# A fused attention, MoE and SwiGLU kernel whose order of work comes from a planner: new durations, lags and due times, the single block last, another order of the seven products

## The chip, the cores and the metric

The kernel runs on one core of a Trainium2 chip. The metric is the device time of one execution in microseconds (us). Inputs and outputs are in device memory; nothing is done on the host.

## What is computed

Three stages follow each other on 4608 tokens of width 512. In the reference:

```python
# 1: linear attention, q, k, v of 8 batches x 8 heads x 576 x 64
q_s = softmax(q, axis=-1); k_s = softmax(k, axis=2)      # over the head's 64, over the 576 rows
kv = einsum('bhsd,bhse->bhde', k_s, v)
x = einsum('bhsd,bhde->bhse', q_s, kv)                   # then heads beside each other: 4608 x 512
# 2: hard swish
h = x @ w_in                                             # 512 -> 2048
y = (h * clip(h + 3, 0, 6) / 6) @ w_out                  # 2048 -> 512
# 3: RMS norm and SwiGLU
xn = y / sqrt(mean(y * y) + 1e-6) * rms_g
out = (silu(xn @ w_gate) * (xn @ w_val)) @ w_out2        # 512 -> 1536 -> 512
```

The softmaxes subtract the maximum first. The four weight matrices arrive as 64-bit floats; the kernel makes 32-bit floats of them with integer operations.

## The kernel before, in words

**Tiling.** The tokens are nine blocks (j = 0 to 8) of 512 columns; the chunks of a width are 128 rows. Each product of two 32-bit matrices is done by three passes of TensorE: operands are split into a high part (a copy into a rounded type by ScalarE, `hi_of`, L201) and a low part (the difference, a tensor_tensor of VectorE or GpSimd, `lo_of`, L207), and high x high, high x low and low x high are added up in PSUM.

**Stages on TensorE.** `m1` (L600) makes h for blocks 0 to 2 with plain products; `prod1` (`product`, L830) makes it for blocks 3 to 8 with seven products in place of eight (a Strassen-Winograd scheme on 256-column halves). `m2` (L659) makes y: 16 steps of 12 matmuls a block. `prod` (L848) makes gate and value for "supers", blocks taken in pairs (two columns of the scheme are two blocks, 512-column matmuls) or a single one (256-column halves). There are 6 chunk pairs i and two matrices z in a super, so 12 groups of seven products; a product is 6 matmuls. `m4` (L968) makes the output: 12 steps of 12 matmuls a block. Before the change the supers are `(0,), (1,2), (3,4), (5,6), (7,8)`.

**The seven products.** They are done in `ORDER` = 1, 6, 5, 2, 7, 3, 4 and accumulate in three PSUM banks x, y, z. Between them sums are taken from PSUM: p1 (ScalarE copies bank x after 1, L863), u2 (VectorE adds bank y after 6, L870), v (VectorE adds bank z after 5), c22 (v plus bank y after 7), c12 and c21. Product 2 waits for p1, 7 for u2, 3 for v, 4 for c22. `merge` strews other steps between the seven: two steps stand behind the fourth and the seventh product, four behind the second, fourth, sixth and seventh.

**The written order of TensorE.** `seq` is a list of all steps of `m1`, `m2`, `prod1`, `prod` and `m4`. In prod1, a block's `m2` steps follow its products by four chunks, and its last four stand in the first group of the next block. In prod, the list `wait` of the m4 steps (super by super, block by block) is eaten two steps a group, whenever the chunks that they need were made by an earlier group; what remains stands at the end.

**The planner.** `Plan` is a list scheduler that runs when the program is built. Every piece of work is a task with an engine, a duration in us, a due time (a place in `seq`), needs, a lag until its result is seen by another engine, and what it takes and gives of pools of buffers ("u": 77 tiles of 128x512; "w": 8 tiles twice as wide; "ps": 4 PSUM banks; "v", "vt", "st"). `emit` goes through simulated time, and gives each free engine the ready task with the smallest due time. The simulated time itself is then forgotten: what remains in the program is the order of instructions on each engine, and that each engine takes them in this order. A VectorE task may go to GpSimd where `other` says so (FLEX), and a task with `port` keeps the two engines apart in the plan. All DMAs are issued by SyncE, in the plan's order; a DMA task lasts 0.73 us there and has a lag of `DMA_LAG` = 2.3 us.

**Attention side work.** `kv_tasks` makes a batch's key-value product: five loads of k, `k_max` (L347: a tensor_reduce over the four rows of a partition; the tail rows L353), a transpose on TensorE (`k_tr`, L363), `k_red` (L367 the maximum of each column; L369 a product with the identity, "kd"), `k_all` (L375: ones x kd, which gives the maximum to all partitions), `k_ev` (L379, ScalarE), `k_sub`, `k_exp`, `kv_mm` (L408), `kv_div`. `q_tasks` makes the query's side: `q_max1` (L500), `q_exp1` (L506), sums (L511, L512), `q_norm` (L516), `q_tr` (L528), and the x products (L548, L556). The norm of block j is `y_ev` (L672, L674: the four PSUM banks of y are copied out, which the next block's first `m2` waits for), squares and sums, `y_sum` (L689) and `y_newton` (L700 to L703).

**Weights.** `weight` plans the conversion of one 128x512 piece: a load into a "w" tile, `conv_a` (two ScalarE operations, L245 and L246), `conv_d` (on VectorE, four operations each in two halves of 256 columns: L254, L256, L258, L262), `conv_p` (L267, GpSimd first) and `conv_s` (L271). There are 68 pieces: "in" 16, "out" 16, "gv" 24 (gate and value), "out2" 12. The 36 last are due one after the other from the first `m2` of block 2 to the fourth group of block 8's prod1; an "out2" piece is then stored (`w_put`) and loaded again (`w_get`) in the prod stage, and split there (`v_hi`, `v_lo`). For the supers of two blocks, the x of the prod stage is loaded into "w" tiles (`load_xn`), 1024 columns at a time.

Of the kernel before, what the change touches and what calls it, by code (L numbers as in the profile page):

```python
# [20 lines left out]
UNITS = 98 - 5 - 2 * WIDE  # L21
# [6 lines left out]
LAG = 3  # L28
SOLO_US, WORTH = 0.2, 0.6
XP = 4  # L30
# [6 lines left out]
class Plan:  # L37
# [5 lines left out]

    def __init__(self, room):
        self.room = dict(room)
        self.tasks = {}

    def add(self, name, engine, us, fn, *args, needs=(), due=0.0, take=(), give=(), spare=0, lag=0.1, other=None, port=True):
        assert name not in self.tasks, name
        self.tasks[name] = (engine, us, fn, args, list(needs), due, dict(take), dict(give), spare, lag, other, port)  # L50

    def emit(self):
# [25 lines left out]
        while len(begun) < len(self.tasks):  # L78
            for engine, heap in ready.items():
# [3 lines left out]
                while heap:  # L83
# [4 lines left out]
                    first, us, fn, args, _, _, take, give, spare, lag, other, port = self.tasks[name]  # L88
# [30 lines left out]
            while events and events[0][0] <= now:  # L119
                _, _, name, far, give = heapq.heappop(events)  # L120
                for p, n in give.items():
                    self.room[p] += n
                for u in users[far].get(name, ()):
                    left[u] -= 1
                    if not left[u]:
                        arm(u)
# [3 lines left out]
def kernel(  # L130
# [35 lines left out]
    SUPER = [(0,), *((j, j + 1) for j in range(1, NJ, 2))]  # L166
    COUPLES = ((1, 6), (5, 2), (7, 3), (4,))
# [26 lines left out]
    g_sb = const.tile([P, C], F32, name="g_sb")  # L194

# [43 lines left out]
    HS = [slice(z * NB // 2, (z + 1) * NB // 2) for z in range(2)]  # L239
# [9 lines left out]
    def conv_d(kind, i):  # L249
# [7 lines left out]
        for h in HS:  # L257
            nc.vector.scalar_tensor_tensor(  # L258
                wi[:, h], t[:, h, 1], -(1 << 30), mi[:, h], ALU.bitwise_and, ALU.bitwise_or
            )  # L260
        for h in HS:
            nc.vector.tensor_scalar(mi[:, h], wi[:, h], -(1 << 23), None, ALU.bitwise_and)  # L262
# [79 lines left out]
    def k_max(b, u):  # L342
# [3 lines left out]
        if u < C:  # L346
            nc.vector.tensor_reduce(  # L347
                m[:, u * P:(u + 1) * P].rearrange("p (h d) -> p h d", h=2),
                kch[b, u].rearrange("p (h t d) -> p h d t", h=2, t=T),
                AX.X, ALU.max,  # L350
            )
        else:
            nc.vector.tensor_max(m[:TAIL], m[:TAIL], kch[b, u][:TAIL])  # L353
# [11 lines left out]
    def k_red(b):  # L365
        m = stat.tile([P, C, 1], F32, tag="kx", bufs=2, name=f"kx{b}")
        nc.vector.tensor_reduce(m, kmp.pop(b), AX.X, ALU.max)  # L367
        kms[b] = utile(f"kd{b}", F32, (P, C, P))
        nc.vector.tensor_tensor(  # L369
            kms[b], ident.rearrange("p (o q) -> p o q", o=1).to_broadcast([P, C, P]), m.to_broadcast([P, C, P]), ALU.mult  # L370
        )

    def k_all(b):
        kmp[b] = ptile(f"kmb{b}")
        nc.tensor.matmul(kmp[b], ones, kms.pop(b).rearrange("p c q -> p (c q)"), start=True, stop=True)  # L375

    def k_ev(b):
        kms[b] = utile(f"kmb{b}")
        nc.scalar.copy(kms[b], kmp.pop(b))  # L379
# [355 lines left out]
    ORDER = (1, 6, 5, 2, 7, 3, 4)  # L735
# [142 lines left out]
    def load_xn(S, k, t):  # L878

        n = f"b{k + 1}{t + 1}"  # L880
        if len(SUPER[S]) == 2:
            x = wtile(f"x{n}_{S}", F32, (P, 2, NB))
            src = xn_d[SUPER[S][t]][2 * k:2 * k + 2]
        else:
            x = utile(f"x{n}_{S}", F32, (P, 2, HALF))
            src = xn_d[SUPER[S][0]][2 * k:2 * k + 2, :, t * HALF:(t + 1) * HALF]
        nc.sync.dma_start(x, src.rearrange("c p t -> p c t"))
        xb["u", S, n] = x

    def u_sum(S, n, x, y, eng):  # L890

        to = {"t3": "b12", "t4": "t2"}.get(n)
        if to:
# [593 lines left out]
```

## Time and profile before

| what | us |
|---|---|
| time of three executions | 1794.81 median (1789.85 to 1899.04) |
| the profiled execution | 1790.45 |
| its span, from the first to the last instruction | 1788.6 |
| TensorE busy in the span | 1711.6 |
| VectorE busy | 1303.7 |
| ScalarE busy | 870.0 |
| GpSimd busy | 260.1 |

The profile is of one execution. The mean granted clock of TensorE in it was 0.988 of full speed. Busy shares are taken over the whole span; waits and windows of the trace show the stretches. The matmul durations of the rows overlap each other, so a busy TensorE need not be one without a loss.

### The profile page before, as it was taken

The page shows a single profiled execution, that of the slowest core. Times are in us where ns is not written, and L with a number is a line of the kernel's source. Part 1 is how long each engine was busy: PE and PEld are TensorE (multiplying, and loading weights), DVE is VectorE, ACT ScalarE, POOL GpSimd, SP SyncE. Part 2 cuts the span into 40 slices and gives each one's busy share as a digit, 9 for nine tenths or more (in the row PEclk, how much of TensorE's full clock was granted, in tenths as well). Part 3 has the DMA queues.
Part 4 walks back from the last instruction along what each step waited for, and adds up shares of the span by engine and source line. Part 5 has one row for each costly group of instructions (what it writes and reads, how often), then busy time and mean ns, then how long its engine had stood idle before and what let it go on. Part 6 is the DMA issues. An engine that isn't in the chain of part 4 may idle for free.

```text
span 1788.6 us, 26411 instructions
## 1 busy us (share of the span) xinstructions
PE 1711.6 (96%) x9150; PEld 1445.5 (81%) x9150; DVE 1303.7 (73%) x2501; ACT 870.0 (49%) x2018; POOL 260.1 (15%) x259
## 2 busy tenths in 40 slices
PE   5899989999999999999999989999999999999999
PEld 3677767888888788898988878878887888788887
DVE  8898977887887888887877786676557655665552
ACT  7865555564564656544546553343234323433331
POOL 3244411021111211121110010020002000100000
PEclk9899999999999999999999999999999999999999
DMA  9547386895887979686793745344354444544443
GB/s 262 174 142 238 115 292 207 308 320 194 269 260 237 269 233 309 213 274 217 266 321 113 244 134 184 109 159 167 122 166 164 159 135 151 173 150 139 147 148 129
DMA packets 192294, 358.27 MB, mean 200 GB/s; under 512 B 26145, under 2 KB 90145, under 8 KB 192161
## 3 DMA queue, kind: packets, MB, share of 16 engines
q1 hardware_dynamic: 192160, 356.59, 61.3%
q8 instruction: 72, 1.18, 0.3%
q14 instruction: 62, 0.50, 0.1%
HBM read 288.88 MB, written 67.63 MB: 199 GB/s over the span
## 4 chain that ended last, share of the span: by engine, by line
PE 74%; DVE 12%; DMA 8%; ACT 3%; issue 2%; SPq 1%; POOL 0%; DVEq 0%; ACTq 0%; POOLq 0%
PE y L659 16%; PE o L968 16%; PE puy L848 12%; PE pux L848 8%; PE puz L848 8%; PE phy L830 4%; PE h L600 3%; PE phz L830 3%; PE phx L830 2%; DMA q<-in_q_dram 2%; DMA raw_gv<-in_moe_w_val_dram 2%; PE kvp L408 2%; DMA raw_out<-in_moe_w_out_dram 1%; ACT q L506 1%; DMA v<-in_v_dram 1%
## 5 line engine op out<-in xcount | busy, mean ns | idle before, releaser
L968 PE MATMUL o<-wv,uh 128*128 128x512 f32 x864 | 267.2, 391 | 0.0
L207 DVE TENSOR_TENSOR plu<-pg,phu 128x512 fp32r<-128x512 f32 (+1 forms) x232 | 149.1, 647 | 122.0 <-ACT phu L201 121.8
L968 PEld LDWEIGHTS o<-wv,uh 128*128 128x128 f32 x864 | 162.4, 189 | 33.2
L968 PE MATMUL o<-wv,ul 128*128 128x512 f32 x432 | 168.7, 390 | 1.0 <-DVE ul L207 1.0
L659 PE MATMUL y<-gh,hout 128*128 128x512 f32 x360 | 144.9, 403 | 10.2 <-DVE ysb L674 9.5
L863 ACT COPY c21u<-pux 128x512 f32<-128x512 f32 (+1 forms) x60 | 32.6, 543 | 241.8 <-PE pux L848 241.7
L659 PE MATMUL y<-gl,hout 128*128 128x512 f32 x360 | 142.6, 396 | 6.2 <-DVE gl L207 5.8
L201 ACT ACTIVATE phu<-pg 128x512 fp32r<-128x512 f32 x240 | 133.5, 570 | 23.1 <-DMA pg<-pd 23.0
L659 PE MATMUL y<-gh,wo 128*128 128x512 f32 x432 | 142.8, 391 | 0.0
L659 PE MATMUL y<-gh,lout 128*128 128x512 f32 x360 | 141.8, 394 | 0.0
L848 PE MATMUL puy<-xhu,phu 128*128 128x512 f32 (+1 forms) x360 | 134.3, 373 | 7.7 <-DVE c22u L870 7.6
L848 PE MATMUL puy<-xlu,phu 128*128 128x512 f32 (+1 forms) x360 | 132.6, 368 | 0.0
L848 PE MATMUL puy<-xhu,plu 128*128 128x512 f32 (+1 forms) x360 | 132.4, 368 | 0.0
L870 DVE TENSOR_TENSOR c22u<-c22u,puy 128x512 f32<-128x512 f32 (+1 forms) x60 | 38.0, 633 | 128.9 <-PE puy L848 128.7
L830 PE MATMUL phy<-xhh,wh 128*128 128x256 f32 x576 | 118.6, 289 | 0.0
L830 PEld LDWEIGHTS phy<-xhh,wh 128*128 128x128 f32 x576 | 95.2, 192 | 3.1 <-issue 1.5
L935 POOL TENSOR_TENSOR u<-u,c12u 128x512 f32<-128x512 f32 x19 | 30.6, 1608 | 458.2 <-DVE c12u L870 286.4
L968 PEld LDWEIGHTS o<-wv,ul 128*128 128x128 f32 x432 | 81.4, 188 | 18.6 <-DVE ul L207 1.5
L659 PEld LDWEIGHTS y<-gh,wo 128*128 128x128 f32 x432 | 81.3, 188 | 15.9
L506 ACT ACTIVATE q<-q,qm 128x64 f32<-128x64 f32 x256 | 85.2, 338 | 15.7 <-DVE qm L500 12.7
L848 PE MATMUL pux<-xlu,phu 128*128 128x512 f32 (+1 forms) x240 | 89.1, 371 | 2.0 <-DVE xlu L207 2.0
L848 PE MATMUL pux<-xhu,phu 128*128 128x512 f32 (+1 forms) x240 | 89.0, 371 | 1.5 <-ACT c21u L863 0.9
(252 smaller groups left out, 4573.8 us busy)
## 6 DMA issues: line engine op xcount, KB each, us to landing
wh<-rdh SPq DMA_DIRECT2D x126, 512.0 KB, 5.2
wv<-rdout SPq DMA_DIRECT2D x96, 512.0 KB, 4.7
pg<-pd SPq DMA_DIRECT2D x180, 256.0 KB, 3.7
wo<-rdout SPq DMA_DIRECT2D x54, 512.0 KB, 4.3
raw_out<-in_moe_w_out_dram SPq DMA_DIRECT2D x28, 512.0 KB, 5.3
rdh<-hw SPq DMA_DIRECT2D x21, 512.0 KB, 4.1
v<-in_v_dram SPq DMA_DIRECT2D x72, 128.0 KB, 5.4
xn_d<-ysb SPq DMA_DIRECT2D x36, 256.0 KB, 4.2
```

Source lines behind the costliest of these rows:

```text
L201: nc.scalar.activation(hi, src, AF.Copy)
L207: on(engine).tensor_tensor(lo, src, hi.bitcast(F32), ALU.subtract)
L408: nc.tensor.matmul(ps[e * D:(e + 1) * D, u, s:s + D + 1], kk, vv, start=(u == 0 and t == 0), stop=(t == T), skip_group_check=True,)
L506: nc.scalar.activation(t, t, AF.Exp, bias=m[:, g, :], accum_out=sm[:, g, :])
L600: nc.tensor.matmul(hps[j, i], w[a][:, o:o + P], xs[j][b][u], start=(u == 0 and m == 0), stop=(u == C - 1 and m == 2),)
L659: nc.tensor.matmul(acc[j][c], w[a][:, c * P:(c + 1) * P], g[b], start=(i == 0 and n == 0), stop=(i == NF - 1 and n == 2),)
L830: nc.tensor.matmul(ps[:, z, :], w[a][:, o:o + P], x[b][:, c * HALF:(c + 1) * HALF], start=(first and z == 0 and c == 0 and m == 0), stop=( ...
L848: nc.tensor.matmul(ps, w[a][:, c * P:(c + 1) * P], x[b][c], start=(first and c == 0 and m == 0), stop=(c == 1 and m == 2), skip_group_chec ...
L863: nc.scalar.copy(cs[l, j, i, "c21"], bank(l, j, i, "x"))
L870: nc.vector.tensor_tensor(cs[l, j, i, n], t, bank(l, j, i, b), ALU.add)
L935: on(eng).tensor_tensor(u, u, c_part("u", S, (i, 1), m, t, 0), ALU.mult)
L968: nc.tensor.matmul(acc["o", j][c], u[a][:, c * P:(c + 1) * P], w[b], start=(i == 0 and n == 0), stop=(i == NF2 - 1 and n == 2),)
```

## The change

It changes the planner's figures, the list `seq`, and a few pieces of computation:

- Planner: `DMA_LAG` 2.3 to 4.0 (and 2 more for loads of q and v), default lag 0.1 to 0.15, TensorE lag 0.2 to 0.25; several durations (conv_d 1.88 to 1.55, conv_a 1.06 to 1.13, GpSimd's 1.23 to 1.35, kv_div 1.25 to 1.48 and others). A task may have `slack`: it is made ready that long after its needs are met. The attention's TensorE tasks from batch 3 (block 3) on get 0.8 us of it (`SIDE`), and `y_sum` too.
- First block: q, v, the first weights and the first query maxima have earlier due times.
- `SUPER` is `(0,1), (2,3), (4,5), (6,7), (8,)`. Block 1 of the first pair fetches its w_out2 parts from device memory as later blocks do.
- `ORDER` is 1, 6, 5, 7, 2, 3, 4, with `COUPLES` to match, and `merge` has fixed places: two steps stand behind the third and the sixth product, four behind the third, fifth, sixth and seventh.
- `m2` follows prod1 by six chunks (`TRAIL`), and no m4 step is given to the last three groups (`REST`).
- "out2" weights are loaded and converted from 30 steps before their first use, without store and second load. "gv" weights are due over a longer stretch, to 16 steps before the last pair's first group in the first super.
- `conv_d` works on whole 512 columns.
- `k_max` takes two tensor_max (256 and 128 columns a partition) in place of the reduce. `k_red` keeps only the maximum; `k_all` is four transposes of the maximum, broadcast along the free axis.
- x of the prod stage is loaded, summed and split in 512-column tiles of the "u" pool, which has 76 tiles now.

```diff
-UNITS = 98 - 5 - 2 * WIDE
+UNITS = 97 - 5 - 2 * WIDE
+SIDE = 0.8
+TRAIL = 6
+REST = 3
...
-                    if not left[u]:
+                    if left[u]:
+                        continue
+                    if self.tasks[u][12]:
+                        heapq.heappush(events, (now + self.tasks[u][12], serial, u, 2, {}))
+                        serial += 1
+                    else:
                         arm(u)
...
-    SUPER = [(0,), *((j, j + 1) for j in range(1, NJ, 2))]
-    COUPLES = ((1, 6), (5, 2), (7, 3), (4,))
+    SUPER = [tuple(range(j, min(j + 2, NJ))) for j in range(0, NJ, 2)]
+    COUPLES = ((1, 6), (5, 7), (2, 3), (4,))
...
-        for h in HS:
-            nc.vector.tensor_scalar(m[:, h], m[:, h], F64_MIN, F64_MAX, ALU.max, ALU.min)
-        for h in HS:
-            nc.vector.tensor_scalar(mi[:, h], mi[:, h], 3, 0x3FFFFFFF, ALU.logical_shift_left, ALU.bitwise_and)
...
+        nc.vector.tensor_scalar(m, m, F64_MIN, F64_MAX, ALU.max, ALU.min)
+        nc.vector.tensor_scalar(mi, mi, 3, 0x3FFFFFFF, ALU.logical_shift_left, ALU.bitwise_and)
+        nc.vector.scalar_tensor_tensor(wi, t[:, :, 1], -(1 << 30), mi, ALU.bitwise_and, ALU.bitwise_or)
+        nc.vector.tensor_scalar(mi, wi, -(1 << 23), None, ALU.bitwise_and)
...
-            nc.vector.tensor_reduce(
-                m[:, u * P:(u + 1) * P].rearrange("p (h d) -> p h d", h=2),
-                kch[b, u].rearrange("p (h t d) -> p h d t", h=2, t=T),
-                AX.X, ALU.max,
-            )
+            t4 = kch[b, u].rearrange("p (h t d) -> p h t d", h=2, t=T)
+            nc.vector.tensor_max(km2, t4[:, :, :T // 2], t4[:, :, T // 2:])
+            nc.vector.tensor_max(m[:, u * P:(u + 1) * P].rearrange("p (h d) -> p h d", h=2), km2[:, :, 0], km2[:, :, 1])
...
-        nc.tensor.matmul(kmp[b], ones, kms.pop(b).rearrange("p c q -> p (c q)"), start=True, stop=True)
+        for c in range(C):
+            nc.tensor.transpose(kmp[b][:, c, :], m[:, c, :].to_broadcast([P, P]), ident)
...
-    ORDER = (1, 6, 5, 2, 7, 3, 4)
+    ORDER = (1, 6, 5, 7, 2, 3, 4)
...
-        out = []
-        for n, p in enumerate(ps):
-            out.append(p)
-            out += ms[n * len(ms) // len(ps):(n + 1) * len(ms) // len(ps)]
-        return out
+        at = {2: (2, 5), 4: (2, 4, 5, 6), 6: (1, 2, 3, 4, 5, 6)}.get(len(ms), range(len(ms)))
+        return [x for n, p in enumerate(ps) for x in (p, *(m for m, a in zip(ms, at) if a == n))]
...
-            late = [(m2, j, i) for i in range(4 * p - 4, 4 * p)] if p else tail2[j - 1]
+            late = [(m2, j, i) for i in range(max(0, 4 * p - TRAIL), 4 * p - TRAIL + 4)] if p else tail2[j - 1]
...
-    FLEX = (G, 1.23)
-    DMA_US, DMA_LAG = 0.73, 2.3
+    FLEX = (G, 1.35)
+    DMA_US, DMA_LAG = 0.73, 4.0
...
-            plan.add((n, "put"), Q, DMA_US, w_put, *n, needs=[(n, "s")], due=d, give=U, lag=DMA_LAG)
-            plan.add((n, "get"), Q, DMA_US, w_get, *n, needs=[(n, "put"), *late[1]], due=h - 5, take=U, spare=5, lag=DMA_LAG)
-            split((n,), [(n, "get"), *step(h - 8)], h - 4, v_hi, v_lo, (i,), first={"w": 1}, take=(), give=U, other=FLEX)
+            split((n,), [(n, "s"), *step(h - 8)], h - 4, v_hi, v_lo, (i,), first={"w": 1}, take=(), give=U, other=FLEX)
...
-            plan.add(have[b], Q, 2 * DMA_US if two else DMA_US, load_xn, S, k, t,
-                     needs=[(y, "store", 2 * k), (y, "store", 2 * k + 1), *step(e - 14)], due=e - 10,
-                     take=R, spare=0 if two else SPARE // 2, lag=DMA_LAG)
+                plan.add(b, Q, DMA_US, load_xn, S, k, t, c,
+                         needs=[*((y, "store", 2 * k + m) for m in ([c] if two else [0, 1])), *step(e - 16)], due=e - 11,
+                         take=U, spare=SPARE // 2, lag=DMA_LAG)
...
+        first, last = pos[m2, 2, 0], pos[prod, 0, NP2 - 1, 0, 1] - 16
+        for z, (m, c) in enumerate(((1, 0), (1, 1), (0, 0), (0, 1))):
+            d = first + (last - first) * (4 * i + z) // (4 * NP2)
+            weight("gv", (i, m, c), pos[prod, 0, i, 0, 1], step(d - 20), (d, ()))
+        for ch in (i, i + NP2):
+            h = pos[m4, 0, 0, ch]
+            weight("out2", ch, h, step(h - 30), (h - 12, ()))
```

## Rows read from the trace of the kernel before

**Rows 1.** The page's first part: busy time, share, instructions of each engine.
```profile
PE 1711.6 (96%) x9150; PEld 1445.5 (81%) x9150; DVE 1303.7 (73%) x2501; ACT 870.0 (49%) x2018; POOL 260.1 (15%) x259
```

**Rows 2.** Stages by windows: length, then busy time (count) by engine, clock, DMA.
```profile
0.00:36.80 36.80, 18.24 (x110) 11.44 (x110) 29.68 (x65) 26.91 (x92) 10.59 (x36) 1.00 1.04 268
36.80:146.00 109.20, 96.67 (x526) 75.16 (x524) 101.43 (x238) 75.34 (x225) 40.27 (x36) 0.92 0.54 163
...
358.00:940.00 582.00, 563.79 (x3713) 500.40 (x3712) 477.47 (x1014) 322.99 (x823) 99.00 (x106) 0.99 0.81 260
940.00:1049.00 109.00, 103.18 (x680) 93.73 (x679) 84.61 (x173) 62.51 (x129) 2.29 (x2) 1.00 0.55 182
...
1204.00:1386.00 182.00, 180.62 (x796) 148.93 (x795) 111.47 (x171) 67.45 (x128) 18.05 (x12) 1.00 0.47 157
```

**Rows 3.** Waits of PE: line <- releaser: us in total, times, longest us.
```profile
PE kmt L363 <- DVE km L353: 10.9, 1, 10.9
PE y L659 <- DVE ysb L674: 9.5, 3, 8.7
PE puy L848 <- DVE c22u L870: 7.6, 6, 2.3
PE kmb L375 <- DVE kd L369: 6.3, 4, 2.8
PE y L659 <- DVE gl L207: 5.8, 5, 1.8
PE kvp L408 <- DVE g L643: 4.5, 3, 1.8
PE kvp L408 <- DMA v<-in_v_dram: 3.6, 1, 3.6
```

**Rows 4.** Groups of PE by line and shape: busy us, mean ns, idle before.
```profile
L375 PE MATMUL kmb<-kd,ones 128*128 128x512 f32 x16 | 11.7, 824 | 7.0 <-DVE kd L369 6.3 <-DMA q<-in_q_dram 0.7
...
L363 PE MATMUL kmt<-ident,km 128*128 128x128 f32 x32 | 5.3, 293 | 10.9 <-DVE km L353 10.9
```

**Rows 5.** Groups of DVE by line and shape: busy us, mean ns, idle before.
```profile
L347 DVE TENSOR_REDUCE km<-k 128x128 f32<-128x512 f32 x32 | 33.6, 1065 | 7.0 <-DMA k<-in_k_dram 6.8
...
L271 DVE TENSOR_TENSOR w_gv<-w_gv,wl_gv 128x512 f32<-128x512 f32 x23 | 15.8, 685 | 3.7 <-POOL wl_gv L267 3.7
...
L369 DVE TENSOR_TENSOR kd<-ident,kx 128x512 f32<-128x512 f32 x8 | 5.5, 692 | 0.4
...
L870 DVE TENSOR_TENSOR c12u<-c21u,puy 128x256 f32<-128x256 f32 x12 | 5.0, 418 | 14.5 <-PE puy L848 14.5
```

**Rows 6.** Chain of waits, window 250 to 272: start us, us, what.
```profile
254.06 6.71 DMA gr<-g_d
...
260.78 5.42 DMA wg_in<-wd_in
...
267.53 1.76 DVE swh L756
```

**Rows 7.** Timeline of PE, window 250 to 272: start us, us.
```profile
270.04 0.77 PE L659 MATMUL y<-gh,hout 128*128 128x512 f32 x1 [8.65 <-DVE ysb L674]
270.60 0.63 PE L659 MATMUL y<-gl,hout 128*128 128x512 f32 x1
```

**Rows 8.** Timeline of DVE, one conversion in halves, start to next task.
```profile
22.09 0.48 DVE L254 TENSOR_SCALAR wm_in<-wm_in 128x256 f32<-128x256 f32 x2
...
24.01 0.17 DVE L511 TENSOR_SCALAR qs<-qs 128x8 f32<-128x8 f32 x1
```

**Rows 9.** Timeline of DVE, three operations each of which needs the last.
```profile
323.44 0.69 DVE L701 SCALAR_TENSOR_TENSOR ra<-rs,ra 128x512 f32<-128x512 f32 x1
324.16 0.43 DVE L702 TENSOR_SCALAR ra<-ra 128x512 f32<-128x512 f32 x1
324.62 0.69 DVE L703 TENSOR_TENSOR r<-r,ra 128x512 f32<-128x512 f32 x1
```

**Rows 10.** Chain of waits at the end: fifteen m4 steps.
```profile
1743.61 40.81 PE o L968 x180
```

More of the change, by code (lines that the diff above doesn't have):

```diff
@@ L46, in __init__, with add @@
         self.tasks = {}
[L48 removed]
+    def add(self, name, engine, us, fn, *args, needs=(), due=0.0, take=(), give=(), spare=0, lag=0.15, other=None, port=True, slack=0.0):
         assert name not in self.tasks, name
[L50 removed]
+        self.tasks[name] = (engine, us, fn, args, list(needs), due, dict(take), dict(give), spare, lag, other, port, slack)
     def emit(self):
@@ L87, in emit @@
                         continue
-                    first, us, fn, args, _, _, take, give, spare, lag, other, port = self.tasks[name]
+                    first, us, fn, args, _, _, take, give, spare, lag, other, port, _ = self.tasks[name]
                     shared = port and engine in ("dve", "pool")
@@ L964, in m4 @@
             ]
-        w, u = wo.pop(("v", S, t, i)) if S else [wt["out2", i][:, z] for z in range(2)], us.pop((S, t, i))
+        w, u = wo.pop(("v", S, t, i)) if S or t else [wt["out2", i][:, z] for z in range(2)], us.pop((S, t, i))
         for c in range(C):
@@ L1064, in weight @@
         elif kind != "gv":
-            split((n,), [(n, "s" if late is None else "get")], h - 4, w_hi, w_lo, n, give=() if kind == "in" else U, other=FLEX)
+            split((n,), [(n, "s" if late is None else "get")], d if first else h - 4, w_hi, w_lo, n, give=() if kind == "in" else U, other=FLEX)
         if kind == "in":
@@ L1125, in q_tasks @@
                      give={"u": 1, "st": 1}, other=FLEX)
-            plan.add((n, "tr"), E, 0.45, q_tr, j, u, needs=[(n, "norm")], due=e - (8 - u) * f, take=PS, give=U, lag=0.2)
+            plan.add((n, "tr"), E, 0.43, q_tr, j, u, needs=[(n, "norm")], due=e - (8 - u) * f, take=PS, give=U, lag=0.25, slack=SIDE * (j > 2))
             bs = [b for _, _, b, _ in runs(j)]
@@ L1177, in xn_tasks @@
         for r, x, y, more in (("t1", "b12", "b11", ()), ("t2", "b22", "t1", ()), ("t3", "b22", "b12", ["t1"]),
                               ("t4", "b21", "t2", [6])):
-            plan.add((n, r), V, us, u_sum, S, r, x, y, needs=[have[m] for m in (x, y)] + [have[m] if m in have else (n, m, "lo") for m in more],
-                     due=e - 3 if r != "t4" else pos[prod, S, 0, 0, 6], take=R if r in ("t1", "t2") else (), other=flex)
-            have[r] = (n, r)
+            for c in range(1 + two):
+                plan.add((n, r, c), V, 0.61, u_sum, S, r, x, y, c,
+                         needs=[have[m, c] for m in (x, y)] + [have[m, c] if (m, c) in have else (n, m, c, "lo") for m in more],
+                         due=e - 3 if r != "t4" else pos[prod, S, 0, 0, 6], take=U if r in ("t1", "t2") else (), other=FLEX)
+                have[r, c] = (n, r, c)
@@ L1182, in xn_tasks @@
         after = {1: ["t1"], 2: ["t4"], 3: ["t2", "t3"], 4: ["t4"], 5: ["t2"], 6: [], 7: []}
         for k in ORDER:
-            last = []
             for c in range(1 + two):
-                nm = (n, k) if c == two else (n, k, c)
-                split(nm, [have[m] for m in (XSRC[k], *after[k])] + last + step(e - XLEAD), pos[prod, S, 0, 0, k] - 4,
-                      u_xhi, u_xlo, (S, k, c), give=R if c == two and k != 6 else (), other=FLEX)
-                last = [(*nm, "lo")]
+                split((n, k, c), [have[m, c] for m in (XSRC[k], *after[k])] + step(e - XLEAD), pos[prod, S, 0, 0, k] - 4,
+                      u_xhi, u_xlo, (S, k, c), give=U if k != 6 else (), other=FLEX)
@@ L1405 @@
             took = 1.37 if len(SUPER[a[0]]) == 2 else 0.72
-        plan.add(st, E, took, f, *a, needs=needs, due=h, take=take, give=give, lag=0.2)
+        plan.add(st, E, took, f, *a, needs=needs, due=h, take=take, give=give, lag=0.25)
     plan.add("gain", Q, 0.3, lambda: nc.sync.dma_start(g_sb, rms_g.rearrange("(c p) -> p c", p=P)), needs=[(m1, 0, 0)])
```

132 lines of the change are left out of this document (54 added, 78 removed).

## The prediction

> **What bounds the kernel now.** I read the page's busy shares first, then the stages by windows, then TensorE's waits, and went to the chain and the timelines only where a wait was long. TensorE is busy 1711.6 of 1788.6 us [rows 1], so only some 77 us of the span are empty, and work that merely moves between the other engines is worth nothing by itself. The windows say where the empty time lies [rows 2]: 18.6 of the first 36.8 us (where the first `m1` starts), 12.5 of the next 109 us, 18.2 of the 582 us of prod1, 5.8 of the 109 us of the single super, but only 1.4 of 182 us in a super of two blocks. VectorE is nearly full in the two first windows (29.7 of 36.8, 101.4 of 109.2), at 477 of 582 us in prod1, and has room only in the supers of two (111.5 of 182). The granted clock is 0.92 in the second window and 1.00 in the supers: stretches with gaps lose a little more than the gaps. The waits [rows 3] name the places: the first key chain (10.9), one evacuation of y (8.7 of 9.5), sums c22 between the seven products (7.6), the key maximum (6.3), low parts of g (5.8), and the key-value product (4.5 and 3.6). The rest of this text asks which of these the change removes, against the profiled execution's own time, 1790.45 us (1788.6 and 1.85 around it). That is 4 us under the median shown, 1794.81, and agrees with the lowest of the three.
>
> **The change, part by part.**
>
> *Key maximum on TensorE.* The 16 matmuls of 512 columns with ones take 11.7 us [rows 4]; four transposes a batch take the place of two matmuls. The nearest row is the transpose of the key maxima, 32 of them in 5.3 us [rows 4], the same count and shape. This gives 11.7 - 5.3 = 6.4 us. A stationary operand with all columns alike is not in the trace; were its load slow, the bound on this side is that nothing is gained, and on the other a gain of 8. I take 6.4.
>
> *Key maximum on VectorE.* The product with the identity goes: 8 x 0.69 = 5.5 us [rows 5]. The reduce takes 1.07 us [rows 5]; a two-input operation of 256 columns takes 0.42 [rows 5], and the second has half the columns, so two cost at most 0.84 and, if the second cost half, 0.63. The 32 reduces then give back 7 to 14 us; I take 11. Of both, what counts is what stands on a chain that TensorE waits for: four waits for kd sum to 6.3 us [rows 3], and 0.69 of each goes, 2.8 us. The Trainium skill, page SBUF — State Buffer, section "Who interferes with whom", speaks against this part: a VectorE instruction with two SBUF inputs contends with GpSimd's reads, a reduce does not. Here one two-input sum took 1.76 us [rows 6] where 0.69 is usual [rows 5], which would fit that rule; by it an unlucky tensor_max costs an estimated 1.1 us more, and a handful of them eat part of the 11 us, not the 2.8.
>
> *Conversion of weights in one width.* In halves a piece takes 24.01 - 22.09 = 1.92 us [rows 8]. In full width each of the four needs the one before. A chain of such operations shows 324.16 - 323.44 = 0.72 us for a scalar_tensor_tensor and 324.62 - 324.16 = 0.46 for a tensor_scalar [rows 9], so the new piece costs 3 x 0.46 + 0.72 = 2.10, or 2.0 if the last one is followed by other work. The planner's new figure, 1.55, is below both. I take +0.1 us a piece, 7 us over 68 pieces, from -0.3 (the planner right) to +0.2. The Trainium skill, VectorE: DVE Perf Modes, section "The DRAIN you can't avoid" and its rules for authors, says to lower the count of operations because each one is followed by the same flush. By that rule four flushes fewer make the piece cheaper; the rows say that an operation that needs the last starts after its end (0.72 after 0.69), and halves avoid just that. By the rule the change would be some 1 to 2 us faster at the start; I stay with the rows.
>
> *Lags and durations.* A wait of 8.65 us before block 1's first `m2` [rows 7] comes from order, not from load: VectorE's copies of y stood behind work that waited for loads, g at 254.06 (6.71 us) and a weight at 260.78 (5.42 us) [rows 6]. The plan believes 0.73 + 2.3 = 3.0 us from issue to sight; it will believe 4.7, which puts such work later in the queue and the copy before it. I take the wait as gone, and with it the slow matmuls behind it (0.43 apart, 270.60 to the next, against 40.81 / 180 = 0.227 [rows 7, 10]; about eight of them, 1.6 us): 9 us together, 4 if a shorter wait remains. The other waits of this kind are low parts of g (5.8) and the key-value product behind g's product (4.5) [rows 3]; the 0.8 us of slack for side work, and a VectorE in prod1 that has 17 conversions fewer (next but one), should take half of these and one half of the remaining kd wait: 7 us, from 0 to 12.
>
> *The start.* The first chain is k loads, maxima, kmt at 10.9, then kd, kmb and five subtractions. Out of it go 0.69 (kd), about 1 (kmb: 2 x 0.82 against 5.3 / 8 [rows 4]) and some 0.4 (the last reduce). The v loads are due before the second pair of weights, which bears on 3.6 us of waiting for v [rows 3]. VectorE, 93% busy up to 146 us [rows 2], gets back 3 batches x (4 x 0.34 + 0.69) = 6 us and gives about 2 to the wide conversion. I take 8 us of the 31 empty ones, from 0 to 15.
>
> *The seven products.* Product 4 had only product 3 (6 matmuls, 6 x 0.227 = 1.4 us [rows 10]) between itself and 7; now 2, 3 and often an `m4` step (12 x 0.227 = 2.7 us) stand there. This bears on the 7.6 us of c22 [rows 3]. What is late next is u2, which has 5 alone ahead of 7, or 5 and a step where steps are strewn in. In the groups that have none (7 of 12 in the first super), u2 must be made in 1.4 us by a VectorE with a queue; so I take 5 us of the 7.6, from -3 to 7.
>
> *Single block last, weights later.* TensorE's work is the same. The end stays as it is: 8 `m4` steps (22 us) in place of 15 (40.81 [rows 10]) still cover the last sums. The first super becomes a pair: 12 groups x 7 products x 1.36 = 114 us, and 16 steps of `m2` and `m4` x 2.72 = 44 us, 158 in all. VectorE's own work in a super of two is 111.5 us [rows 2], less 14 low parts of u that come only later (14 x 0.69 = 10): 102. Into it come 12 "out2" and, by the due times (342 planner steps, 68 of them behind prod1, 24 pieces), 5 "gv" conversions: 17 x (2.0 + 0.69) + 12 x 0.69 = 54 us. That is 156 of 158 us, fuller than any stretch of the trace but the first, though GpSimd, 2.3 us busy in the present first super [rows 2], can take a part. The windows with VectorE over 90% lost TensorE 11% and more [rows 2]; the supers lost 1%. I take a tenth of the 102 us difference in the middle: 8 us more than now, from 0 to 54. In exchange prod1 loses 17 x 2.6 = 44 us of VectorE's 477, which is the cover for the 7 us above. SyncE loses 24 transfers, hidden on both sides.
>
> *x in the shared pool.* A super needs 8 loads and 4 sums in "u" tiles that were "w" tiles, and each load wants 9 free ones of 76. I take 2 us over four borders, from 0 to 4 x 8.65 (the one long wait that late inputs made here [rows 7]).
>
> Sum: -6.4 - 2.8 - 9 - 7 - 8 - 5 + 8 + 2 = -28.2; the wide conversion stands in the start. 1790.45 - 28.2 = 1762 us.
>
> **The rivals.**
>
> *All of it goes.* The waits of rows 3 that no chain needs vanish, and the first super finds GpSimd free. Of the 77 empty us [rows 1] some 25 stay (the first loads and key chain); with the 6.4 that is 1790.45 - 52 - 6.4 + 0 = 1732 us. For it: nothing but order makes most of these waits. Against: every order so far made some.
>
> *A new order, as many waits.* The plan forgets its time, and new figures deal the waits out anew. Only the transposes stay: 1784 us. For it: the waits of rows 3 are short and many, six a kind. Against: the longest two have one cause each, and both are addressed.
>
> *VectorE is full in the first super.* Place: the first pair. Price: the 54 us of conversions wait on nothing else and push the low parts that products wait for. The gains outside are 28 + 10 = 38; once more than 38 of the 54 show, the kernel is slower, and with all of them 1790.45 - 38 + 54 = 1806 us. For it: 156 of 158 us. Against: conversions are due 12 steps before their use, and GpSimd is idle there.
>
> **How the numbers follow.** Forecast 0.52, with its own range 1745 to 1778; all goes 0.23; as many waits 0.17; VectorE full 0.08. To leave no more than two in ten outside, the range takes half of the second case and nearly all of the third: 1738 to 1794. Two per cent is 36 us, about what a measurement of this kernel can tell from no change. Faster by that, under 1755: the second case and a fifth of the forecast, 0.33. Slower by that, over 1826: 0.03, the tail of the last. The rest, 0.64, is within.
>
> **What would show it.** Right: L375 in 32 transposes and near 5 us; no wait for ysb over 2 us; c22 waits under 3 us; the first `m1` before 33 us (now at 36.8); the windows of the supers still within 2% of TensorE's work. Wrong: a long wait for xlu or plu at the borders of supers or in the first, waits for u2 (c12u) in place of c22, or a wide conversion of 1.6 us, which would make the start faster than I say. The forecast fails as a whole if TensorE's busy time itself changes by more than 10 us.

## The result, and the profile after

The changed kernel takes 1768.78 us (median of four, 1766.21 to 1773.87) where the kernel before, beside it, takes 1792.33: a ratio of 0.988, 95% interval 0.984 to 0.991; one execution of the kernel before, at 1899.04 us, is left out of the ratio. The profiled executions are 1766.21 and 1790.45 us, their spans 1764.3 and 1788.6. So 24 us went between the profiled executions and 22 by the ratio, where the sum said 28; the median is 7 us above the forecast's 1762, and lies in the range and in the forecast's own part of it. Where the 24 us lie is another matter.

The page's first part, of the kernel after (busy time, share of the span, instructions):

```profile
PE 1697.6 (96%) x9166; PEld 1438.2 (82%) x9166; DVE 1294.8 (73%) x2202; ACT 866.3 (49%) x2018; POOL 348.7 (20%) x326
```

Beside [rows 1] TensorE's empty time fell from 77.0 to 66.7 us, and its busy time by 14. Of the 14, 5.8 are the key maximum's matmuls (11.7 to 5.9 us); the other matmuls are the same and took less time, at a mean granted clock of 0.992 instead of 0.988. GpSimd has 89 us more work. The first and last start of three kinds of matmul, kernel after (count, shortest, median and longest ns, first and last start in us); they mark `m1`, `prod1` and `prod`:

```profile
L603 PE MATMUL h<-xh,hin x192: 387/389/795, 34.3 to 240.2; 128*128 128x512 f32 x192
...
L833 PE MATMUL phx<-xhh,phh x96: 277/283/365, 353.9 to 895.1; 128*128 128x256 f32 x96
...
L851 PE MATMUL pux<-xhu,phu x240: 277/389/398, 915.1 to 1736.3; 128*128 128x512 f32 x96, 128*128 128x256 f32 x24
```

The same in the kernel before:

```profile
L600 PE MATMUL h<-xh,hin x192: 387/389/793, 36.8 to 234.7; 128*128 128x512 f32 x192
...
L830 PE MATMUL phx<-xhh,phh x96: 277/283/365, 358.2 to 920.9; 128*128 128x256 f32 x96
```

There `prod` begins at 940.8. Two `m2` steps (5.4 us) now stand behind prod1's first product that stood ahead of it, and two behind `prod`'s first. With that taken out, the part before prod1 got 1.1 us longer (358.2 to 353.9, but 5.4 of work less), prod1 21.4 us shorter (582.6 to 561.1), and the rest 4.0 us shorter. Stages by windows, kernel after (columns as in [rows 2]):

```profile
0.00:34.30 34.30, 15.78 (x113) 11.11 (x113) 26.41 (x55) 26.94 (x93) 6.67 (x31) 1.00 1.02 274
34.30:146.00 111.70, 92.34 (x520) 72.67 (x519) 103.05 (x181) 76.93 (x226) 37.73 (x38) 0.91 0.55 162
354.00:915.00 561.00, 557.05 (x3721) 498.48 (x3720) 447.25 (x810) 309.12 (x801) 103.80 (x109) 1.00 0.78 246
915.00:1086.00 171.00, 162.70 (x705) 131.34 (x705) 165.89 (x253) 92.08 (x168) 67.80 (x46) 1.00 0.54 178
1086.00:1267.00 181.00, 179.52 (x793) 148.32 (x792) 104.41 (x163) 67.60 (x127) 31.29 (x22) 1.00 0.48 161
```

Prod1 has 4.0 empty us where it had 18.2. The second window has 19.4 in place of 12.5. The first super, now a pair, has VectorE busy for 97% of it and 8.3 us empty. The single super at the end has almost none (0.1 of 109 us). TensorE's waits, kernel after (columns as in [rows 3]):

```profile
PE kmt L368 <- DVE qs L514: 13.9, 2, 13.1
PE puy L851 <- DVE c12u L873: 8.3, 7, 2.6
PE kmt L368 <- DVE km L358: 7.8, 1, 7.8
PE kvp L411 <- ACT k L395: 4.5, 2, 3.4
PE kvp L411 <- DMA raw_in<-in_moe_w_in_dram: 4.4, 1, 4.4
PE y L662 <- POOL gl L221: 3.9, 1, 3.9
...
PE puy L851 <- DVE c22u L873: 2.3, 3, 1.3
...
PE y L662 <- DVE gl L221: 0.9, 1, 0.9
...
PE puz L851 <- DVE c22u L873: 0.7, 1, 0.7
...
PE y L662 <- DVE ysb L677: 0.4, 1, 0.4
```

Against [rows 3], the waits for ysb, kd (now kx), c22 and low parts of g by VectorE are nearly gone, or fell to less than half (c22, 2.3 + 0.7). The first key transpose waits 13.1 us where it waited 10.9. New are the waits for u2 of the u products (its tile is `c12u`), a second key chain (7.8), a weight's transfer and a low part of g made by GpSimd (3.9).

### The profile page after: what moved, and what is told of

It is laid out like the page before. It is cut to its first block, busy times and chain, and to the rows that moved or that the text cites. A ratio compares the mean times of both kernels' runs of the same rounds, so it can differ in the third digit from the quotient of the medians.

```text
span 1764.3 us, 26397 instructions
## 1 busy us (share of the span) xinstructions
PE 1697.6 (96%) x9166; PEld 1438.2 (82%) x9166; DVE 1294.8 (73%) x2202; ACT 866.3 (49%) x2018; POOL 348.7 (20%) x326
## 5 line engine op out<-in xcount | busy, mean ns | idle before, releaser
L221 POOL TENSOR_TENSOR plu<-pg,phu 128x512 fp32r<-128x512 f32 (+1 forms) x63 | 85.4, 1356 | 442.5 <-ACT phu L215 403.1
L221 DVE TENSOR_TENSOR ul<-u,uh 128x512 fp32r<-128x512 f32 x100 | 68.6, 688 | 67.0 <-ACT uh L215 45.8
L221 DVE TENSOR_TENSOR plu<-pg,phu 128x512 fp32r<-128x512 f32 (+1 forms) x177 | 115.5, 661 | 0.9 <-ACT phu L215 0.8
L221 POOL TENSOR_TENSOR gl<-g,gh 128x512 fp32r<-128x512 f32 x36 | 53.2, 1483 | 272.2 <-ACT gh L215 212.7
L873 DVE TENSOR_TENSOR c21u<-c21u,puy 128x512 f32<-128x512 f32 (+1 forms) x60 | 37.9, 631 | 82.5 <-PE puy L851 82.5
```

Source lines behind the costliest of these rows:

```text
L221: on(engine).tensor_tensor(lo, src, hi.bitcast(F32), ALU.subtract)
L873: nc.vector.tensor_tensor(cs[l, j, i, n], t, bank(l, j, i, b), ALU.add)
```

## The experiments

Each kernel is compared with the kernel before on the same chip; where two kernels are compared, the difference of their ratios is taken times 1791 us. The two intervals together leave such a difference uncertain by some 7 us. The lengths of stages are from one profile of each kernel: prod1 from its first matmul to the first of `prod`, and `prod` from there to the last matmul of `m4`. TensorE's idle time in a stage is summed from the trace. `TRAIL`, `REST`, the other durations and lags, and x in 512-column tiles were not tried apart.

**Weights early again (after, with the due times, the store and the second load of before).**

```
+ plan.add((n, "put"), ...); plan.add((n, "get"), ...)
- first, last = pos[m2, 2, 0], pos[prod, 0, NP2 - 1, 0, 1] - 16
+ first, last = pos[m2, 2, 0], pos[prod1, NJ - 1, 3, 1]
...
- weight("out2", ch, h, step(h - 30), (h - 12, ()))
+ weight(kind, n, h, step(d - 20), (d, back))
```

> The changed kernel, with the due times of the 36 last weight conversions (and the store and second load of the out2 pieces) as before; all else stays changed. In the changed trace the gain lies in prod1: from the first prod1 to the first prod 561 us against 583. Theory 1 (room on VectorE: 17 conversions fewer in prod1): TensorE's lost time there comes back, the stretch is 572 to 582 us again, and the first super is some 5 us shorter since VectorE is not full there; total 1772 to 1780. Theory 2 (the lags): prod1 stays within 4 us of 561, the first super gets shorter, total 1760 to 1768. Theory 3 (slack of the side work): as theory 2.

1782.94 us, ratio 0.994 (0.992 to 0.996): 12 us of the change's gain go. Prod1 lasts 579.9 us, as before the change, with 14.0 us of idle TensorE; the rest lasts 837.4, 7 us less than in the changed kernel. The two windows (prod1, first super):

```profile
360.20:940.10 579.90, 565.85 (x3721) 503.68 (x3720) 496.88 (x880) 324.44 (x833) 143.64 (x136) 0.99 0.81 263
940.10:1110.00 169.90, 167.20 (x729) 136.00 (x727) 119.61 (x190) 79.62 (x144) 21.09 (x15) 1.00 0.41 138
```

VectorE has 497 us of work in prod1 instead of 447, and 120 instead of 166 in the first super. Load taken off prod1 is worth 19 us there and costs 7 behind it. That is theory 1, with a total 3 us above its range. VectorE's room is not shown to be all of it: of TensorE's waits in prod1 6.5 us are for VectorE, but 2.0 for ScalarE and 2.5 for one load, and the edit gives ScalarE, GpSimd and SyncE more work as well. Prod1 also begins 6 us later here; a_order shows the same with nothing changed ahead of prod1 (last section).

**Old lags (after).**

```
- DMA_US, DMA_LAG = 0.73, 4.0
+ DMA_US, DMA_LAG = 0.73, 2.3
...
- lag=DMA_LAG + 2)
+ lag=DMA_LAG)
```

> The changed kernel with the DMA lag of before (2.3 us, and no 2 more for q and v). Theory 1 (room on VectorE): prod1 within 4 us of 561, total 1764 to 1774. Theory 2 (the lags let nothing stand behind a late load): the long wait for ysb at block 1 (8.65 us before) comes back, with more waits behind loads in prod1, total 1780 to 1790. Theory 3 (slack): as theory 1.

1783.63 us, ratio 0.996 (0.994 to 0.998): 15 us go. Prod1's window, and the longest of TensorE's waits in it:

```profile
352.40:929.40 577.00, 563.49 (x3723) 500.96 (x3722) 444.62 (x815) 308.72 (x801) 90.53 (x97) 0.99 0.75 239
```

```profile
PE phy L833 <- DVE c12h L873: 5.1, 3, 2.3
```

VectorE's wait for the loads of q in prod1, here and then in the changed kernel:

```profile
DVE qm L503 <- DMA q<-in_q_dram: 19.9, 11, 5.2
```

```profile
DVE qm L503 <- DMA q<-in_q_dram: 8.4, 8, 2.3
```

VectorE's load in prod1 is that of the changed kernel (444.6 and 447.3), and yet 13.5 us are empty instead of 4.0. So room on VectorE alone does not give the 21 us. An order that believes loads to be early puts an instruction that still waits at the head of VectorE's queue: the query maximum waits there 19.9 us in all instead of 8.4, and the sums that TensorE needs (c12 of prod1: 5.1 us instead of 1.1) stand behind. That the first makes all of the second was not followed wait by wait. The 8.65 us for ysb [rows 7] did not come back as such: the longest is 1.9. The order deals out the place anew. Theory 2 has the total; of its signs the waits in prod1 came, the long wait for ysb did not.

**No slack for side work (after).**

```
- SIDE = 0.8
+ SIDE = 0.0
```

> The changed kernel with SIDE = 0, so the attention's TensorE tasks are ready as soon as their needs are met in the plan. Theory 3 (slack): the waits of TensorE for the key maximum, the key-value product and the query parts in prod1 come back, 8 to 14 us over five batches; total 1774 to 1782. Theories 1 and 2: under 4 us, total 1765 to 1773.

1772.76 us, ratio 0.989 (0.986 to 0.992). Prod1 lasts 564.3 us, 3 more than in the changed kernel, with 7.7 empty; the time as a whole can't be told from it. The slack is a small part.

**Old order of the seven products, and the old merge (after).**

```
- ORDER = (1, 6, 5, 7, 2, 3, 4)
+ ORDER = (1, 6, 5, 2, 7, 3, 4)
```

> The changed kernel with the order of the seven products, the couples and the places of the strewn steps as before. If the order matters as the prediction had it (5 us of c22 waits): c22 waits of 6 to 9 us instead of the c12u (u2) waits of 8.3, total within 3 us of the changed kernel. A rival, that the order spared prod1 more than the supers (product 4 waited for c22 behind side work there): prod1 5 to 10 us longer, total 1774 to 1780.

1783.16 us, ratio 0.995 (0.993 to 0.997): 12 us go. The `prod` part takes 10.2 us more. Its three longest waits, then the first two supers:

```profile
PE puy L851 <- DVE c22u L873: 11.8, 9, 4.2
...
PE o L962 <- DVE ul L221: 3.1, 1, 3.1
...
PE puy L851 <- DVE c12u L873: 1.0, 1, 1.0
```

```profile
922.90:1093.90 171.00, 159.56 (x677) 128.43 (x676) 158.21 (x245) 87.79 (x159) 54.04 (x39) 0.98 0.52 176
1094.00:1275.00 181.00, 177.08 (x774) 145.87 (x773) 109.12 (x172) 65.24 (x124) 17.60 (x13) 0.99 0.46 157
```

The old order waits 11.8 us for c22 and 1.0 for u2 (`c12u`) where the new one waits 2.3 + 0.7 and 8.3 + 0.4: 12.8 against 11.7 us for both sums. So the order moves this wait from c22 to u2 more than it takes it away; another 3.1 us of the old one are for a low part that `m4` needs. The two first supers have 11.4 and 3.9 empty us where the changed kernel has 8.3 and 1.5: 5.5 of the 10.2 us. The granted clock is 0.98 and 0.99 there instead of 1.00, and 2% of 171 and 1% of 181 us are the other 5. Prod1 itself takes 1.9 us more, so neither theory has the total. Prod1 begins 5.9 us later than in the changed kernel, although TensorE's instructions are the same in the same order up to there. That part is not the order's doing (last section).

**Conversion in halves again (after; the planner's 1.55 stays).**

```
- nc.vector.tensor_scalar(m, m, F64_MIN, F64_MAX, ALU.max, ALU.min)
+ for h in HS:
+     nc.vector.tensor_scalar(m[:, h], m[:, h], F64_MIN, F64_MAX, ALU.max, ALU.min)
...
```

> The changed kernel with the four operations of the conversion in two halves each, as before; the planner's figure stays 1.55. The plan is the same, so every engine has the same order apart from the halves. By the rows an undisturbed piece goes from 1.98 back to 1.89 us. Theory A (full width costs VectorE 0.1 us a piece, and more where GpSimd holds the shared port): the stretch to the last m1, 240.6 us, is 2 to 6 us shorter, total 1762 to 1768. Theory B (a count of operations is what costs): the stretch is 2 to 6 us longer, total 1771 to 1778.

1763.33 us, ratio 0.984 (0.982 to 0.987): 6 us less than the changed kernel, with intervals that overlap, and the profiled executions are alike (1766.76 and 1766.21). The gain is not at the start, where I expected it (the last `m1` matmul is 3 us later): `prod` takes 840.3 us instead of 844.6, and u2 (`c12u`) is waited for 5.0 us instead of 8.3. By itself this run does not show a gain; c_best below repeats it.

**Planner's figure for the conversion 2.0 instead of 1.55 (after).**

```
- plan.add((n, "d"), V, 1.55, conv_d, ...
+ plan.add((n, "d"), V, 2.0, conv_d, ...
```

> The changed kernel with the planner's figure for the conversion at 2.0 us, the measured undisturbed length, in place of 1.55. Theory A (VectorE falls behind a plan that believes 1.55, so TensorE finds its key transpose of batch 1 waiting 7.8 us at 40 us, and more of that kind): that wait falls under 4 us and the last m1 comes 4 to 10 us earlier than 240.6; total 1760 to 1766. Theory B (the plan is only shuffled): the last m1 within 3 us of 240.6 or later, total 1766 to 1778.

1775.86 us, ratio 0.991 (0.989 to 0.993), no better and perhaps 6 us worse. The long wait of the second key chain stays (7.0), and `prod` takes 854.5 us, with 16.1 us of waits for u2 (`c12u`). The truer figure only shuffled the order.

**Old due times of the first block (after).**

```
- due=e - 16 * f + u % C * f if e else -6,
+ due=e - 16 * f + u % C * f,
...
- due=e - (18 - u) * f if e else -7.2 if u else -9, ...
+ due=e - (18 - u) * f, ...
- d = -4.5 if first else d
...
```

> The changed kernel with the due times of the first block (first weights, q, v, first query maxima) as before. Theory A (the new due times put two query maxima and all q loads ahead of k, so the first key transpose came at 13.1 us instead of 10.9): it comes at 9.5 to 11.5 us, the first m1 at 32 to 34, total 1764 to 1769. Theory B (the prediction's: the new due times help v and the first weights): the first m1 at 36 to 38 instead of 34.3, total 1771 to 1776.

1758.67 us, ratio 0.981 (0.979 to 0.984): 11 us less than the changed kernel. Its `m1`, TensorE's wait for the second key chain, and its two longest waits from the last `m1` to prod1:

```profile
L603 PE MATMUL h<-xh,hin x192: 388/389/796, 37.4 to 225.2; 128*128 128x512 f32 x192
```

```profile
PE kmt L368 <- DVE km L358: 1.3, 1, 1.3
```

```profile
PE y L662 <- ACT hw L215: 4.8, 1, 4.8
PE y L662 <- DVE gl L221: 3.9, 4, 1.4
```

The new due times do bring the first `m1` forward, by 3.1 us (34.3 against 37.4). The last `m1` is then 15 us later (240.2 against 225.2): TensorE's idle time between the two is 24.7 us in the changed kernel and 10.9 here. The wait for the second key chain, 7.8 us, is 1.3 here. Not all of the 15 us last: behind the last `m1` this kernel has the 4.8 and 3.9 us above, which the changed kernel has not, and prod1 begins 7.0 us earlier (346.9 against 353.9). The two profiled executions are 6.4 us apart; that the medians are 11 apart is within the uncertainty. Neither theory had both numbers. Which of the due times does it was not tried apart.

**The key maximum alone (the kernel before, with the transposes and the two-step maximum).**

```
- nc.tensor.matmul(kmp[b], ones, kms.pop(b)..., start=True, stop=True)
+ for c in range(C):
+     nc.tensor.transpose(kmp[b][:, c, :], m[:, c, :].to_broadcast([P, P]), ident)
...
```

> The kernel before with the new key maximum alone (two tensor_max for the reduce, no product with the identity, four transposes for the product with ones; one tile fewer), with the planner's figures as before. The prediction's terms: 6.4 us on TensorE and 2.8 us of waits for kd, together 9 us: 1781 to 1785 beside 1791, with the eight key products near 5.3 us busy instead of 11.7. A rival, that these matmuls were hidden in waits that stay: within 3 us of before.

1787.98 us, ratio 0.998 (0.996 to 1.000): 4 us. Its group of matmuls:

```profile
L372 PE MATMUL kmb<-ident,kx 128*128 128x128 f32 x32 | 6.6, 340 | 11.1 <-DVE kx L366 11.1
```

TensorE's work falls as reckoned, from 11.7 to 6.6 us. The wait ahead of it grows from 6.3 to 11.1 us, which spends half the gain. In the longest of these waits, 4.7 us at 48.7, the maximum stands in VectorE's queue behind query maxima, and the last of them waits 2.73 us for its load:

```profile
52.12 0.69 DVE L497 TENSOR_REDUCE qm<-q 128x8 f32<-128x512 f32 x1 [2.73 <-DMA q<-in_q_dram]
52.72 0.68 DVE L366 TENSOR_REDUCE kx<-kmt 128x4 f32<-128x512 f32 x1
```

What is gained lies ahead of prod1, which begins 5.2 us earlier (353.0 against 358.2) and lasts 583.1 us, as before. The total is between the two expectations.

**Longer lags and late weights alone (the kernel before).**

```
- DMA_US, DMA_LAG = 0.73, 2.3
+ DMA_US, DMA_LAG = 0.73, 4.0
...
+ weight("out2", ch, h, step(h - 30), (h - 12, ()))
```

> The kernel before with two parts of the change: the longer DMA lags and the late conversion of the gv and out2 weights; the rest (order of the products, single block first, key maximum, halves, durations) as before. Undoing either of the two in the changed kernel cost 16 and 19 us of the 21 that prod1 had won, so neither does it alone. Theory A (the two together are the prod1 gain): prod1 lasts 562 to 569 us instead of 583, total 1772 to 1780. Theory B (they need the order, the durations or the slack as well): prod1 lasts 572 us or more, total 1780 or more.

1798.06 us, ratio 1.004 (1.003 to 1.006): slower than before. Prod1, and the single super behind it:

```profile
358.80:924.70 565.90, 559.33 (x3714) 499.61 (x3713) 439.87 (x875) 305.12 (x796) 95.51 (x96) 1.00 0.77 243
924.70:1060.00 135.30, 110.10 (x670) 96.22 (x669) 132.64 (x322) 79.04 (x159) 25.57 (x19) 0.95 0.63 216
```

The two edits alone give 16.7 of prod1's 21.4 us, as theory A had it; its total failed. But `prod` grows by 27 us: the single super is too short for the weights that now fall into it, VectorE is busy 98% of the window, and TensorE is empty for 25 us of it.

**The single block first again (after).**

```
- SUPER = [tuple(range(j, min(j + 2, NJ))) for j in range(0, NJ, 2)]
+ SUPER = [(0,), *((j, j + 1) for j in range(1, NJ, 2))]
```

> The changed kernel with the single block first again. VectorE was busy 166 of the first 171 us of the first pair, with waits of 8.3 us at TensorE for u2 (c12u). Theory A (the single block first is worse, since its short groups leave VectorE less time a group): the prod stage is 848 to 860 us instead of 844.6, total 1772 to 1784. Theory B (a single first makes the wait for conversions milder or equal): 838 to 846 us, total 1762 to 1770.

1807.07 us, ratio 1.008 (1.005 to 1.011): 36 us more than the changed kernel. Prod1 keeps its 560.1 us; `prod` takes 878.5 instead of 844.6. The first super:

```profile
917.20:1065.00 147.80, 123.81 (x717) 106.08 (x715) 141.08 (x269) 82.82 (x165) 31.18 (x22) 0.93 0.60 208
```

This is my third rival with its sign, in a single super and not in the pair where I put it; that 1807 is near its 1806 us is luck, since that sum was made for the pair. It is also more than theory A allowed. With the late weights the pair at the head is needed; what it earns without them was not tried apart.

**The best of both (after, with the old due times of the first block and the conversion in halves).**

```
- due=e - 16 * f + u % C * f if e else -6,
+ due=e - 16 * f + u % C * f,
...
+ for h in HS:
...
```

> The changed kernel with two of its parts undone: the due times of the first block and the full width of the conversion. Undone one at a time they gave 10 and 5 us. If they add up: 1750 to 1756. If both touch the same waits before 146 us: 1757 to 1761, the better of the two.

1750.26 us, ratio 0.978 (0.974 to 0.981). Prod1 takes 560.6 and `prod` 840.3 us, and the last `m1` is at 224.2: the two gains (11 and 6 us) add up, 18 us in all. Beside a_start, halves gain 7 us here, and `prod` is 5.9 us shorter (840.3 against 846.2). With a_halves that is twice the same way: halves pay, by some 6 us, though neither run alone proves it.

**The same, with the gate and value weights due within prod1 again.**

```
- first, last = pos[m2, 2, 0], pos[prod, 0, NP2 - 1, 0, 1] - 16
+ first, last = pos[m2, 2, 0], pos[prod1, NJ - 1, 3, 1]
```

This is the last due time of "gv" as the kernel before has it; "out2" stays late.

> As c_best, and the gv conversions are due up to the fourth group of block 8's prod1 as before the change, only the out2 conversions in the first super. Theory A (VectorE full in the first super costs TensorE 5 us or more there): the prod stage is 3 to 6 us shorter than c_best's and prod1 no more than 2 us longer, total 1 to 4 us under c_best. Theory B (prod1 needs the room more): prod1 5 us or more longer, total above c_best.

1747.56 us, ratio 0.976 (0.973 to 0.978), the fastest version, 44 us under the kernel before; its first super:

```profile
902.60:1072.00 169.40, 166.20 (x725) 135.46 (x724) 149.01 (x281) 90.26 (x165) 60.37 (x40) 1.00 0.49 165
```

VectorE is at 149 of 169 us instead of 165, and prod1 does not suffer (560.7). `prod` is 1.7 us shorter, less than theory A had. The difference to the version above lies within the intervals. So with the old due times and the halves, prod1 does not need the later due times of the gate and value weights: those of "out2", which also lose their store and second load, are enough.

## Why the prediction was right, and where its steps were not

The total is 7 us off because errors of both signs cancelled. By its own terms, some 22 us were forecast before prod1 (start, ysb, half of the key maximum), 12 in prod1, and 5 lost in `prod`. Measured: 1 lost, 21 gained, 4 gained. So the time was met by luck: no stage came out as forecast.

*Key maximum.* Right in its parts. TensorE's and VectorE's groups, kernel after:

```profile
L378 PE MATMUL kmb<-ident,kx 128*128 128x128 f32 x32 | 5.9, 314 | 0.8 <-DVE kx L372 0.8
...
L368 PE MATMUL kmt<-ident,km 128*128 128x128 f32 x32 | 5.8, 313 | 21.7 <-DVE qs L514 13.9 <-DVE km L358 7.8
```

```profile
L355 DVE TENSOR_TENSOR km<-k 128x256 f32<-128x256 f32 x32 | 14.4, 449 | 4.4 <-DMA k<-in_k_dram 3.9
...
L356 DVE TENSOR_TENSOR km<-km 128x128 f32<-128x128 f32 x32 | 10.3, 322 | 1.2
```

5.9 us for 5.3 forecast, and the stationary operand with equal columns costs no more than a plain transpose (314 and 313 ns). On VectorE 33.6 [rows 5] became 24.7, a gain of 9 for 11. The price that the rule of the Trainium skill (SBUF — State Buffer, "Who interferes with whom") put on the two-input maximum does show. VectorE, kernel after:

```profile
39.59 0.42 DVE L355 TENSOR_TENSOR km<-k 128x256 f32<-128x256 f32 x1
40.05 1.24 DVE L356 TENSOR_TENSOR km<-km 128x128 f32<-128x128 f32 x1
41.32 1.44 DVE L355 TENSOR_TENSOR km<-k 128x256 f32<-128x256 f32 x1
42.80 0.29 DVE L356 TENSOR_TENSOR km<-km 128x128 f32<-128x128 f32 x1
```

and GpSimd in the same stretch:

```profile
39.82 1.32 POOL L274 TENSOR_TENSOR wl_in<-wl_in,wm_in 128x512 f32<-128x512 f32 x1 [3.45 <-DVE wm_in L269]
41.22 1.26 POOL L278 TENSOR_TENSOR w_in<-w_in,wl_in 128x512 f32<-128x512 f32 x1
```

The two middle ones, 0.29 and 0.42 us by themselves, end 0.15 and 0.28 us after the GpSimd instruction beside them (39.82 + 1.32 and 41.22 + 1.26). With that the rule agrees. At 0.42 and 0.29 us each, 32 pairs would take 22.7 us, so such meetings took 2 of the 11 us. As to what the whole edit brings, b_key says 4 us (0.5 to 8) on the plan of before, against 9 for its two terms. What it brings in the new order was not tried.

*The wide conversion.* Right in sign, and smaller than forecast. One undisturbed piece, kernel after, from the first to the next task:

```profile
15.15 0.37 DVE L266 TENSOR_SCALAR wm_in<-wm_in 128x512 f32<-128x512 f32 x1
15.56 0.43 DVE L267 TENSOR_SCALAR wm_in<-wm_in 128x512 int32<-128x512 int32 x1
16.02 0.69 DVE L268 SCALAR_TENSOR_TENSOR w_in<-raw_in,wm_in 128x512 int32<-128x512 int32 x1
16.75 0.43 DVE L269 TENSOR_SCALAR wm_in<-w_in 128x512 int32<-128x512 int32 x1
17.09 0.68 DVE L391 TENSOR_TENSOR k<-k,kmb 64x512 f32<-64x512 f32 x1
```

17.09 - 15.15 = 1.94 us (the next undisturbed one takes 1.98), where I said 2.0 to 2.1 and halves take 1.92 [rows 8]. Each operation starts 0.03 to 0.04 us after the end of the one that it needs; the last is followed 0.09 us before its recorded end by one that doesn't need it. The rule to keep the count of operations low (the Trainium skill, VectorE: DVE Perf Modes, "Rules for kernel authors") would have this piece cheaper; the trace does not bear that out (1.94 us against 1.92), and the halves are some 6 us faster (a_halves, c_best).

*Lags and durations.* The wait for ysb went (8.7 to 0.4), as I had it, and from the last `m1` to prod1 TensorE's idle time fell from 8.7 to 3.4 us. The total before prod1 fell short because up to the last `m1` the idle time grew, from 33.7 to 43.2 us, where the start term had 8 us less. The terms for prod1 (7, and half of the key maximum) came to some 12 where 21.4 were measured, and b_key shows that the key maximum alone gives prod1 nothing (583.1 us). The step that failed is what I credited. I gave half of the short waits to the slack and VectorE's room together, and the lags only the wait for ysb. The slack is worth some 3 us there (a_noside); the lags act in prod1 as much as the room does. Without the room 14.0 us of idle time stay, without the lags 13.5, with both 4.0.

*The start.* This term failed in sign: 8 us gained were forecast, and the new due times cost 11 by the ratios, 7 where prod1 begins. I priced what goes out of the first chain and took the first `m1` as the measure. It came 2.5 us sooner (34.3, not under 33). What else is due before time zero (q and v loads, the first weights) was counted as relief; a_start shows that it pushes the second key chain back, and TensorE waits for it once the first `m1` matmuls are done. VectorE is 90% busy up to 146 us before and 89% after (the prediction's 93% is that of the second window alone), so work that it takes early probably leaves other work late.

*The seven products.* c22's 7.6 us fell to 3.0, and u2 (`c12u`) rose to 8.3, the sign of failure that I had named. With the old order the kernel is slower, by 10 us in `prod`, half of them idle time and half a lower granted clock. So the 5 us of the term can be seen in the idle time, but not for its reason: the sums c22 and u2 together are waited for 12.8 us in the old order and 11.7 in the new one. How much of it would remain without the late weights was not tried.

*The first super.* 8.3 us empty for 5.8 of the single super before. I had taken 8 more (a tenth of 102 us, as the prediction works it, would be 10). VectorE did come to 166 of 171 us, more than reckoned (156 of 158), and GpSimd took 68. Why the loss stayed small is not shown; that the conversions are due long before use, as I had argued against my rival, would fit it. The rival holds where the window is shorter: a_super and b_both.

*x in the shared pool.* No wait for x appears in the waits of `prod`; the 2 us were not spent.

## What to carry to other kernels

Where a program fixes the order of in-order queues, a figure in its planner acts through what stands at the head of a queue when its data is late: give loads the lag that the trace shows, and judge the order by waits, not by the figure's truth (a truer duration gave nothing here, longer lags some 15 us). Moving work off a full stretch pays only if the stretch that receives it has room on the same engine, so price both together: the same late weights gain here with a pair of blocks behind them and lose with a single one. A first matmul that starts sooner says nothing about the stage; look at where the next stage starts, since even the last matmul of this one was 15 us off where 7 remained.

## What the runs showed of the hardware that was not expected

In a_order TensorE has the same instructions in the same order as the changed kernel up to prod1, but prod1 begins at 359.8 instead of 353.9 us. The windows up to there, the changed kernel and then a_order (columns as in [rows 2]):

```profile
0.00:353.85 353.85, 307.23 (x1556) 244.65 (x1557) 294.97 (x498) 215.54 (x565) 89.09 (x108) 0.96 0.66 212
```

```profile
0.00:359.75 359.75, 311.38 (x1556) 247.71 (x1557) 295.67 (x499) 216.34 (x565) 88.89 (x108) 0.93 0.64 208
```

Idle time accounts for 1.8 us of the 5.9; the other 4.2 are the same 1556 matmuls taking longer, at a mean granted clock of 0.93 instead of 0.96. a_halves has that order too, and is at 311.4 us busy with a clock of 0.95. All have gaps in this stretch, and in full windows of the supers the clock is 1.00, its upper level, in every run. The mean clock does differ between executions of one kernel: it is 0.988 to 0.992 in the four of the changed kernel, and the profiled one is the fastest, with 0.992. That chance puts the difference into this stretch is likely, not shown. A few us of the start are not to be credited to an edit on one profile.
